# Expert 0's third rows transposed into the bank of the transposed k, and VectorE's lower parts placed ahead of the counts and the list of empty slots

## The chip, the cores and the metric

The kernel runs on one core of a Trainium2 chip. The core has a matrix engine (TensorE, PE in the profile, with its weight loads shown as PEld), a vector engine (VectorE, DVE), a scalar engine (ScalarE, ACT), a general engine (GpSimd, POOL) and an engine that here only issues transfers (SyncE, SP). Each engine works through its own instructions in order, and waits on semaphores for what others have to finish first. The metric is the device time of one execution in microseconds; less is better.

## The reference

Two parts are joined. The first is a retention layer over 8 batches, 8 heads, 576 positions and 64 columns per head: scores q k^T / 8, multiplied by a decay that is zero above the diagonal, times v. The second is a mixture of 8 experts over the 4608 resulting rows of 512 columns; each row goes to the one expert with the largest gating logit.

```python
scores = scale * np.matmul(q, k.transpose(0, 1, 3, 2))
ret = scores * Dmat[None, :, :, :]
attn_out = np.matmul(ret, v)
...
logits = x @ w_gate
e_idx = np.argmax(logits, axis=1)
gate_w = probs[np.arange(N), e_idx]
eom = 1.0 / (1.0 + np.exp(-(x @ w_output_gate)))
for e in range(E):
    mask = e_idx == e
    h = np.maximum(x[mask] @ w1[e], 0.0)
    ye = h @ w2[e]
    out[mask] = gate_w[mask, None] * eom[mask, e, None] * ye
```

## The kernel before

The rows are cut into 36 tiles of 128 (`NTILE`), in groups of four (`GT`), nine groups in all. **Stage one** is the loop over `g` from 0 to 35 (lines 580 to 640). In one turn TensorE forms the scores of tile g+1 into the PSUM tile `sc` (two banks, line 303), the part of tile g that comes from the running state and then the part from its own scores, both into `o_ps` (`by_state`, `outT`), the new state (`update`, not for the last tile of a batch), the transposed k of the next tile into the bank `k_ps` (`k_rows`, not for every tile), and the natural rows and gating logits of tile g-1 into the banks `xa` and `xb` (`xnat`). VectorE masks the scores out of `sc`, scales `o_ps` into `xT`, and adds up the logits. ScalarE empties `xa` and `xb` into `xgrp`.

After every fourth tile a group's gating runs: `gate1a` and `gate1b` find the expert of each row, `gate2` counts ranks on TensorE into the `k_ps` bank, `gate3a` forms the slot of each row, `gate3b` finishes the row's weight and adds the group's counts to `cum`. From the slots GpSimd scatters the group's rows into the DRAM array `xs`, which is sorted by expert (`scatter_x`, line 194, through the list `todo`). Groups 5 and 7 also set `gt["fill"]`, and `gate4` then lists expert 0's empty slots (`fill`, lines 207 to 218), into which GpSimd scatters the zero rows `zx`. The group that this text speaks of is group 7, whose slots are formed in turn 34.

**Stage two** is the experts: the rows come back from `xs`, transposed to columns, and each value is split into a higher part (`xh`, written by ScalarE, line 241) and the remaining lower part (`xl`, written by VectorE, line 245), so that three products replace one. `transp_hi` transposes and writes the higher part, `transp_lo` the lower. `mm1` (line 262) is the first matrix product of an expert, `mm2` (line 283) the second. Expert 0 starts early: the first `TA` = 3 row tiles of its slots (128, 128 and 104 rows) are loaded in turn 31, and transposed in turns 33, 34 and at the start of turn 35. TensorE's transposes go into a PSUM bank that `pools["x_ps"]` names: the `k_ps` bank in turn 33, `sc[:, 1]` in turn 34, `sc[:, 0]` in turn 35.

The order on every engine in the loop is that of the program text (`manual_schedule`). From turn 34 on the order before the change is:

- TensorE: `outT(34)`, `update(34)`, `gate2` of group 7, `xnat(33)`, transposes of rows 1, transposes of rows 2, `by_state(35)`, `outT(35)`, `xnat(34)`, then `mm1(0,0,0)`, `mm1(0,0,1)`, `xnat(35)` and more products.
- VectorE: `xT(34)` (line 422), `gate3a` (lines 478 to 485), logits of tile 33 (540, 541), `gate3b` (495 to 507), `gate4` (515, 207 to 218), `xl` of rows 1, `xl` of rows 2, `xT(35)`, logits of tile 34, then the hidden layer's lower parts (line 270).
- GpSimd: at the end of turn 35 it issues all of `todo` (line 636): four scatters of group 7's rows and three of zero rows, with a memset of a work tile ahead of each.

After the loop `gate3a` and `gate3b` run again for group 8 (lines 709, 710). Line 487 makes its slots (line 485) wait for every scatter issued so far, and the count on TensorE at line 717 needs its `cum` (line 507). The four PSUM buffers `h_ps` of `mm1` lie where the tiles of stage one lay.

Of the kernel before, what the change touches and what calls it, by code (L numbers as in the profile page):

```python
# [10 lines left out]
F32 = mybir.dt.float32  # L11
# [15 lines left out]
P = 128  # L27
NP = H // 2
NTILE = NT // P
# [11 lines left out]
GT = 4  # L41
# [7 lines left out]
def tile_retention_moe(  # L49
# [49 lines left out]
    cum = const.tile([P, E], BF16, name="cum")  # L99
# [5 lines left out]
    def load_rest(step):  # L105
        if step < 3:
            n = slice(P * (step + 2), P * (step + 3))
            SP.dma_start(out=gq_sb[:, :, n], in_=gq[:, :, n])
        if step == 0:
            for p in range(NP):  # L110
                o = 0 if p % 2 == 0 else 16
                A.copy(out=iw[:, p, o:o + P], in_=ident)
        elif step == 1:
            SP.dma_start(out=con_sb[:, CPB * H + 3 * P:], in_=cmat[:, CPB * H + 3 * P:])
        elif step == 2:
            SP.dma_start(out=cbf_sb, in_=cbf)
            SP.dma_start(out=csm_sb, in_=csm)
            SP.dma_start(out=tok_sb, in_=tokid)
            for x in xgrp:
                G.memset(x[:, :, DM:XW], 0.0)  # L120
            G.memset(zx.bitcast(I32)[:, DM:DM + 1], NT)
# [37 lines left out]
    pools = {"xt0": xta, "ht0": hpa}  # L159
# [61 lines left out]
    def transp(e, t):  # L221
        transp_lo(*transp_hi(e, t))

    def transp_hi(e, t):
        part, n = (0, TA * P) if t < TA else (1, CAP - CA)
        t0 = t if part == 0 else t - TA
        if (e, part) not in XT:
            pl = pools[f"xt{part}"]
            XT[e, part] = (pl.tile([P, KB, n], F32R, name=f"xh{part}"), pl.tile([P, KB, n], F32R, name=f"xl{part}"))
        m = ROWS[t] if e == 0 else P  # L230
        hi, lo = (a[:, :, P * t0:P * t0 + m] for a in XT[e, part])
        if e == 0:
            src = pools["x_ps"]()[:, :, :, 0:m]
            for k in range(KB):
                T.transpose(src[:, k // 2, k % 2, :], XG[e, t][0:m, k:DM:KB], ident[0:m, 0:m])
            hi, lo = (a.rearrange("p (b k) i -> p b k i", b=2) for a in (hi, lo))
        else:
            src = pools["xq"].tile([P, KB, P], F32, name="x_t", bufs=2)
            V.transpose(out=src.rearrange("p k (u j) -> p u k j", u=4),
                        in_=XG[e, t].rearrange("p u (i k) -> p u k i", k=KB))  # L240
        A.copy(out=hi, in_=src)
        return src, hi, lo

    def transp_lo(src, hi, lo):
        V.tensor_tensor(out=lo, in0=src, in1=hi.bitcast(F32), op=ALU.subtract)
# [52 lines left out]
    ps_s = psctx.enter_context(tc.tile_pool(name="ps_s", bufs=1, space=PSUM, side="right"))  # L298

    pk, kn, vs, xT, gt = {}, {}, {}, {}, {}  # L300
    st_ps, stcur = [None], [None]

    sc = ps_s.tile([P, 2, 512], F32, name="sc")
# [32 lines left out]
    def load_k(g):  # L336

        if g < NTILE and g % CPB != 8 and by_rows(g):
            kn[g] = wk.tile([P, DM], F32, name="kn")
            SP.dma_start(out=kn[g], in_=krow[g])  # L340

    def k_rows(g):

        if g % CPB == 8 or by_rows(g):
            return
        ps = ps_s.tile([P, NP, P], F32, name="k_ps")
        for p in range(NP):
            T.transpose(ps[:, p, :], pk[g][:, 1, P * p:P * p + P], ident)
        kn[g] = wk.tile([P, DM], F32, name="kn")
        A.copy(out=kn[g], in_=ps.rearrange("p a i -> p (a i)"))  # L350
# [139 lines left out]
    def gate3b():  # L490
        n, oh, ex, zs = gt.pop("pend")
        sli = gt.pop("sl")
        x = xgrp[n % 2]
        es = sm.tile([P, GT, 1], F32, name="es")
        V.tensor_reduce(out=es, in_=ex, op=ALU.add, axis=AX.X)
        V.tensor_scalar(out=es, in0=es, scalar1=1e-9, scalar2=None, op0=ALU.add)
        V.scalar_tensor_tensor(out=zs, in0=zs, scalar=1.0, in1=es, op0=ALU.add, op1=ALU.mult)
        V.tensor_copy(x.bitcast(I32)[:, :, DM:DM + 1],
                      tok_sb[:, n * GT:(n + 1) * GT].rearrange("p (t a) -> p t a", a=1))
        V.reciprocal(out=x[:, :, DM + 1:DM + 2], in_=zs)  # L500

        todo.extend(partial(scatter_x, x[:, t, :], sli[:, t, :]) for t in range(GT))
        if n == 0:
            V.memset(cum, 0.0)
        ohs = sm.tile([P, E], F32, name="ohs")
        V.tensor_reduce(out=ohs, in_=oh.rearrange("p t e -> p e t"), op=ALU.add, axis=AX.X)
        V.tensor_tensor(out=cum, in0=cum, in1=ohs, op=ALU.add)
        if n in (SNAP, NTILE // GT - 2):
            gt["fill"] = n

    def gate4():
        n = gt.pop("fill")
        if n == NTILE // GT - 2:

            V.tensor_tensor(out=cnt[:, 0], in0=cnt[:, 0], in1=bump, op=ALU.add)
            todo.extend(fill(0, 1, cnt[:, 0:1], lim, CT - TA + 1)[0])
        if n == SNAP:

            todo.extend(fill(0, 1, cnt[:, 0:1], float(CA), TA)[0])
            V.tensor_scalar(out=bump, in0=cnt[:, 0], scalar1=-1.0, scalar2=float(CA), op0=ALU.mult, op1=ALU.add)  # L520
            V.tensor_scalar(out=bump, in0=bump, scalar1=0.0, scalar2=None, op0=ALU.max)
            V.tensor_copy(base2, base)
            V.tensor_tensor(out=base2[:, 0, 0:1], in0=base2[:, 0, 0:1], in1=bump, op=ALU.add)
# [42 lines left out]
    gap = const.tile([1, 1], F32, name="gap")  # L566
    every = {mybir.EngineType.PE, mybir.EngineType.Activation, mybir.EngineType.DVE, mybir.EngineType.SP}

    pools["x_ps"] = lambda: ps_s.tile([P, NP, P], F32, name="k_ps").rearrange("p (b k) i -> p b k i", b=2)
    def scatters(n, pause):  # L570
        for f in todo[0:n]:

            G.memset(pause, 0.0)
            f()
        del todo[0:n]

    with tc.manual_schedule():
        S_next = scores(0)
        k_rows(0)
        for g in range(NTILE):  # L580
            S_sb = S_next
            prev = stcur[0] if g % CPB != 0 else None
            if g < 4:
                load_rest(g)
            load_k(g + 1)
            if g < NTILE - 4:
                load(g + 4)
            if g == GT * SNAP + 11:
                first = list(scat)
            if g == GT * SNAP + 11:  # L590
                for t in range(TA):
                    load_rows(0, t, first)
                load_idx(0, 0, first)
            if g == 0:
                outT(g, S_sb, prev)
            if g + 1 < NTILE:
                prep(g + 1)
                S_next = scores(g + 1)
            else:
                pools["x_ps"] = lambda: sc[:, 0].rearrange("p (b k i) -> p b k i", b=2, k=2)  # L600
                transp(0, 2)
            if g < NTILE - 1:

                scatters(2 if GT * SNAP + 6 < g < GT * SNAP + 11 else 1, gap)
            if prev is not None:
                by_state(g, prev)
            weights(g)
            if g > 0:
                outT(g, S_sb, prev)
            update(g)  # L610
            if "pend" in gt and g % GT == 2:

                gate2(ps_s.tile([P, NP, P], F32, name="k_ps").rearrange("p a i -> p (a i)"))
            if g + 1 < NTILE:
                k_rows(g + 1)

            if "half" in gt:
                gate1b()
            if "fill" in gt:
                gate4()  # L620
            if "ps" in gt:
                gate3a()
            weights_lo(g, (0,))
            weights_lo(g - 1, (1,))
            if g > 0:
                xnat(g - 1)
            if "sl" in gt:
                gate3b()
            if "fill" in gt and g == NTILE - 2:
                gate4()  # L630
            if g % GT == 0 and g > 0:
                gate1a(g // GT - 1)
            if g == NTILE - 1:
                wide = wk.tile([P, H, D], F32, name="vp")
            if g == NTILE - 1:
                scatters(len(todo), wide)
            if g in (NTILE - 3, NTILE - 2):
                if g == NTILE - 2:
                    pools["x_ps"] = lambda: sc[:, 1].rearrange("p (b k i) -> p b k i", b=2, k=2)
                transp(0, g - NTILE + 3)  # L640
    gt["after"] = list(scat)
    psctx.close()
    ps_h = mctx.enter_context(tc.tile_pool(name="ps_h", bufs=4, space=PSUM, side="right", reuse_waits="tile"))
# [148 lines left out]
    with ExitStack() as octx:  # L792
        ov = octx.enter_context(tc.tile_pool(name="ov", bufs=1))
        ps_v = octx.enter_context(tc.tile_pool(name="ps_v", bufs=2, space=PSUM))
        n = nc.values_load(ovn[0:1, 0:1], min_val=0, max_val=NOV)  # L795
        with tc.For_i(0, n, 1) as i:
# [3 lines left out]
            x = ov.tile([P, XW], F32, name="ox")  # L800
# [14 lines left out]
            oh = ov.tile([P, FB, P], F32, name="ohT")  # L815
# [83 lines left out]
```

## Time and profile before

| | us |
|---|---|
| median of 3 runs | 612.72 |
| lowest and highest of them | 611.83, 613.25 |
| the profiled execution | 608.3 |
| its span, first to last instruction | 606.5 |
| PE busy in the span | 591.2 |
| DVE busy | 332.0 |
| ACT busy | 221.3 |
| POOL busy | 188.0 |

The span is what the trace covers; the profiled execution took 1.8 us more than that. A row of the timeline gives the start in microseconds from the start of the span, the time taken, the engine, the line, the operation, the tile written and the tiles read, the shape, and in brackets how long the engine had been idle before it and whose work ended that idle time. The view of windows gives the busy time of each engine in a stretch, and the granted clock of TensorE (PEclk), where 1.00 is full speed.

### The profile page before, as it was taken

How to read it: one execution, taken by the hardware profiler on the slowest of the kernel's cores; microseconds unless marked ns; L12 is line 12 of the kernel's file. 1: busy time of each engine (PE TensorE's matmuls, PEld its weight loads, DVE VectorE, ACT ScalarE, POOL GpSimd, SP SyncE). 2: the span in 40 equal slices, each digit the busy share in tenths (PEclk: the TensorE clock that was granted, in tenths of full speed). 3: DMA queues.
4: the chain of work that ended last, by engine and by line, in shares of the span. 5: the costliest groups of instructions: out<-in, count | busy, mean ns of one | idle time of the engine just before them, and what ended most of it. 6: DMA issues, size and time to landing. Idle time of an engine off the chain costs nothing. (4 is left out here: it accounts for less than half of the span.)

```text
span 606.5 us, 13987 instructions
## 1 busy us (share of the span) xinstructions
PE 591.2 (97%) x5688; PEld 529.4 (87%) x5688; DVE 332.0 (55%) x731; ACT 221.3 (36%) x481; POOL 188.0 (31%) x235
## 2 busy tenths in 40 slices
PE   8899999999899999999999999999999999999995
PEld 6789889889798999879978987997899799889974
DVE  3498989898460666625543554445265435625410
ACT  3233444333231544325333443443354344325110
POOL 2245555575636524016013301601250110110011
PEclk9999999999799999999999999999999999999998
DMA  9988999995215676434343634444262335321011
GB/s 312 356 306 329 322 308 328 346 308 165 90 57 192 177 198 194 140 118 135 110 138 116 175 104 136 116 139 139 96 189 91 121 102 146 100 83 52 1 38 42
DMA packets 56925, 100.28 MB, mean 165 GB/s; under 512 B 14839, under 2 KB 35832, under 8 KB 56860
## 3 DMA queue, kind: packets, MB, share of 16 engines
q1 hardware_dynamic: 46988, 76.72, 39.9%
q0 software_dynamic: 9440, 21.60, 9.8%
q8 instruction: 45, 0.74, 0.5%
q10 hardware_dynamic: 432, 1.05, 0.5%
q14 instruction: 20, 0.16, 0.1%
HBM read 77.75 MB, written 31.18 MB: 180 GB/s over the span
## 5 line engine op out<-in xcount | busy, mean ns | idle before, releaser
L262 PE MATMUL h_ps<-xh,w1h 128*128 128x360 f32 (+1 forms) x512 | 155.4, 303 | 0.0
L262 PE MATMUL h_ps<-xh,w1l 128*128 128x360 f32 (+1 forms) x512 | 155.0, 303 | 0.0
L262 PE MATMUL h_ps<-xl,w1h 128*128 128x360 f32 (+1 forms) x512 | 154.9, 303 | 0.0
L289 POOL DMA_INDIRECT out_dram<-y,idx x40 | 39.7, 993 | 314.5 <-ACT y L288 269.5
L270 DVE SCALAR_TENSOR_TENSOR hl<-h_ps,hh 128x360 fp32r<-128x360 f32 (+1 forms) x128 | 61.3, 479 | 129.0 <-ACT hh L269 123.2
L283 PE MATMUL y_ps<-w2h,hh 128*128 128x512 f32 (+1 forms) x320 | 125.1, 391 | 0.0
L283 PE MATMUL y_ps<-w2l,hh 128*128 128x512 f32 (+1 forms) x320 | 125.0, 391 | 0.0
L283 PE MATMUL y_ps<-w2h,hl 128*128 128x512 f32 (+1 forms) x320 | 124.7, 390 | 0.0
L269 ACT ACTIVATE hh<-h_ps 128x360 fp32r<-128x360 f32 (+1 forms) x128 | 54.7, 427 | 118.0 <-PE h_ps L262 117.1
L262 PEld LDWEIGHTS h_ps<-xl,w1h 128*128 128x128 f32 x512 | 96.3, 188 | 0.3
L262 PEld LDWEIGHTS h_ps<-xh,w1h 128*128 128x128 f32 x512 | 96.3, 188 | 0.3
L262 PEld LDWEIGHTS h_ps<-xh,w1l 128*128 128x128 f32 x512 | 96.2, 188 | 0.0
L288 ACT ACTIVATE y<-y_ps,idx 128x512 f32<-128x512 f32 (+1 forms) x40 | 27.5, 688 | 138.8 <-issue 90.1
L147 DVE TENSOR_TENSOR w1l<-st,w1h 128x512 fp32r<-128x512 f32 x64 | 47.3, 776 | 48.2 <-ACT w1h L142 46.8
L283 PEld LDWEIGHTS y_ps<-w2h,hl 128*128 128x128 f32 (+1 forms) x320 | 58.8, 184 | 14.1
L283 PEld LDWEIGHTS y_ps<-w2h,hh 128*128 128x128 f32 (+1 forms) x320 | 58.9, 184 | 13.8
L283 PEld LDWEIGHTS y_ps<-w2l,hh 128*128 128x128 f32 (+1 forms) x320 | 58.8, 184 | 13.6
L354 POOL TENSOR_TENSOR vp<-pk,con_sb 128x512 f32<-128x512 f32 x36 | 37.4, 1040 | 54.5 <-PE st_ps L394 34.9
L194 POOL DMA_INDIRECT xs<-xgrp,sli x36 | 39.0, 1082 | 33.0 <-issue 17.1
L194 POOL DMA_INDIRECT xs<-zx,fill x42 | 45.2, 1077 | 7.1 <-issue 6.6
L147 DVE TENSOR_TENSOR w2l<-st,w2h 128x512 fp32r<-128x512 f32 x64 | 44.7, 736 | 2.3
L378 DVE TENSOR_TENSOR S_sb<-sc,con_sb 128x512 f32<-128x512 f32 x64 | 41.1, 683 | 7.1 <-PE sc L367 6.6
(128 smaller groups left out, 672.4 us busy)
## 6 DMA issues: line engine op xcount, KB each, us to landing
st<-in_w_dram SPq DMA_DIRECT2D x64, 512.0 KB
pk<-in_pack_dram SPq DMA_DIRECT2D x32, 768.0 KB
x_q<-xs SPq DMA_DIRECT2D x140, 64.0 KB
kn<-in_krow_dram SPq DMA_DIRECT2D x14, 256.0 KB
gq_sb<-in_gq_dram SPq DMA_DIRECT2D x5, 256.0 KB
pk<-in_pack_dram SPq DMA_DIRECT2D x4, 256.0 KB
pk<-in_pack_dram SPq DMA_DIRECT2D x2, 512.0 KB
x_g<-xs SPq DMA_DIRECT2D x4, 256.0 KB
```

What stands on the lines that cost most here:

```text
L147: V.tensor_tensor(out=lo[:, k], in0=st[:, k], in1=hi[:, k].bitcast(F32), op=ALU.subtract)
L194: i = G.indirect_dma_start(out=xs, out_offset=bass.IndirectOffsetOnAxis(ap=at, axis=0), in_=x, in_offset=None, **({} if bound is None else ...
L262: i = T.matmul(ps, lhsT=a[:, k, :], rhs=b[:, k, 0:n], start=(j == 0), stop=(j == 3 * KB - 1))
L269: A.activation(out=hh, in_=ps, func=AF.Relu)
L270: V.scalar_tensor_tensor(out=hl, in0=ps, scalar=0.0, in1=hh.bitcast(F32), op0=ALU.max, op1=ALU.subtract)
L283: i = T.matmul(ps, lhsT=a[:, n], rhs=b, start=(j == 0), stop=(j == 3 * FB - 1))
L288: A.activation(out=y, in_=ps, func=AF.Copy, scale=idx.bitcast(F32)[0:m, e, t, 1:2])
L289: G.indirect_dma_start(out=out, out_offset=bass.IndirectOffsetOnAxis(ap=idx[0:m, e, t, 0:1], axis=0), in_=y, in_offset=None, bounds_check= ...
L354: G.tensor_tensor(out=vs[g], in0=pk[g][:, 2].rearrange("p (h d) -> p h d", h=H), in1=gk_sb[:, g % CPB].broadcast_to([P, H, D]), op=ALU.mult)
L378: V.tensor_tensor(out=v(S_sb[:, r].rearrange("p a i -> p (a i)")), in0=v(sc[:, r]), in1=cmat_sb[:, 0:2].rearrange("p c a i -> p a (c i)"). ...
```

## The change

`gate3b` is cut in two. Its end, which adds the group's expert counts to `cum` and sets the mark for the list of empty slots, becomes `gate3c`, called at once except for group 7. For group 7 `gate3b` moves to turn 34's transposes, between `transp_hi` and `transp_lo` of rows 1; `gate3c` and `gate4` move to the end of turn 35, behind `xnat(34)` and just ahead of the scatters. And the transposes of rows 2 at the start of turn 35 go into the `k_ps` bank and no longer into `sc[:, 0]`.

```diff
+        gt["cum"] = (n, oh)
+        if n != NTILE // GT - 2:
+            gate3c()
+
+    def gate3c():
+        n, oh = gt.pop("cum")
         if n == 0:
             V.memset(cum, 0.0)
         ohs = sm.tile([P, E], F32, name="ohs")
...
-    pools["x_ps"] = lambda: ps_s.tile([P, NP, P], F32, name="k_ps").rearrange("p (b k) i -> p b k i", b=2)
+    def k_bank():
+        return ps_s.tile([P, NP, P], F32, name="k_ps").rearrange("p (b k) i -> p b k i", b=2)
+
+    pools["x_ps"] = k_bank
+
...
             else:
-                pools["x_ps"] = lambda: sc[:, 0].rearrange("p (b k i) -> p b k i", b=2, k=2)
+                pools["x_ps"] = k_bank
                 transp(0, 2)
...
-            if "sl" in gt:
+            if "sl" in gt and g != NTILE - 2:
                 gate3b()
-            if "fill" in gt and g == NTILE - 2:
-                gate4()
             if g % GT == 0 and g > 0:
                 gate1a(g // GT - 1)
             if g == NTILE - 1:
                 wide = wk.tile([P, H, D], F32, name="vp")
-            if g == NTILE - 1:
+                gate3c()
+                gate4()
                 scatters(len(todo), wide)
             if g in (NTILE - 3, NTILE - 2):
                 if g == NTILE - 2:
                     pools["x_ps"] = lambda: sc[:, 1].rearrange("p (b k i) -> p b k i", b=2, k=2)
-                transp(0, g - NTILE + 3)
+                x = transp_hi(0, g - NTILE + 3)
+                if "sl" in gt:
+                    gate3b()
+                transp_lo(*x)
```

## The prediction

> **What bounds the kernel now.** I read the page first, then TensorE's waits, then its timeline around the one long wait, then the granted clock there.
>
> ```profile
> span 606.5 us, 13987 instructions
> PE 591.2 (97%) x5688; PEld 529.4 (87%) x5688; DVE 332.0 (55%) x731; ACT 221.3 (36%) x481; POOL 188.0 (31%) x235
> PEclk9999999999799999999999999999999999999998
> ```
>
> TensorE is busy for 97% of the span: what shortens its chain shortens the kernel. Its clock is full in every slice but one in the middle, the eleventh (151.6 to 166.8 us). The waits of TensorE from 138 us to the end, the whole answer:
>
> ```profile
> PE sc L235 <- DVE xl L245: 3.0, 1, 3.0
> PE t_ps L717 <- DVE cum L507: 0.2, 1, 0.2
> ```
>
> One wait of 3.0 us: transposes (line 235) wait for VectorE's lower parts (line 245). After it TensorE waits 0.2 us in 440. So nothing behind 156 us has slack on TensorE to swallow a gain, and loads and scatters that TensorE's progress releases move with it. The place itself, in TensorE's timeline (first a usual turn, then the wait):
>
> ```profile
> 147.04 0.66 PE L531 MATMUL xa<-iw,xT 128*128 128x144 f32 x4
> 148.02 0.67 PE L235 MATMUL k_ps<-con_sb,x_g 128*128 128x128 f32 x4
> 148.61 0.90 PE L367 MATMUL sc<-pk 64*64 64x128 f32 x32
> 149.33 0.62 PE L409 MATMUL o_ps<-pk,stT 64*64 64x128 f32 x16
> 149.88 1.09 PE L418 MATMUL o_ps<-S_sb,vp 128*64 128x128 f32 x16
> 150.81 0.64 PE L394 MATMUL st_ps<-vp,kn 128*64 128x64 f32 x16
> ...
> 151.64 0.74 PE L531 MATMUL xa<-iw,xT 128*128 128x144 f32 x4
> 152.70 0.64 PE L235 MATMUL sc<-con_sb,x_g 128*128 128x128 f32 x4
> 156.30 0.97 PE L235 MATMUL sc<-con_sb,x_g 104*128 104x104 f32 x4 [2.96 <-DVE xl L245]
> ...
> 162.08 0.60 PE L262 MATMUL h_ps<-xh,w1h 128*128 128x360 f32 x1
> 162.51 0.33 PE L262 MATMUL h_ps<-xl,w1h 128*128 128x360 f32 x1
> 162.68 0.33 PE L262 MATMUL h_ps<-xh,w1l 128*128 128x360 f32 x1
> ```
>
> Rows 1 are transposed at 152.70, rows 2 only at 156.30, after 2.96 us idle. And what follows the wait is slow: four transposes take 0.97 us, in the usual turn 0.67. The view of windows says why:
>
> ```profile
> 19.07:22.48 3.41, 2.08 (x60) 1.43 (x52) 1.78 (x4) 0.18 (x1) 0.35 (x1) 1.00 1.09 317
> ...
> 152.20:155.61 3.41, 1.14 (x10) 0.94 (x8) 2.96 (x22) 1.33 (x3) 0.56 (x1) 1.00 0.02 5
> 155.61:159.02 3.41, 2.72 (x28) 2.14 (x30) 1.23 (x3) 0.51 (x1) 3.08 (x5) 0.50 0.42 159
> 159.02:162.44 3.42, 3.42 (x21) 3.09 (x18) 0.87 (x2) 0.37 (x1) 3.09 (x5) 0.50 0.40 158
> 162.44:165.85 3.41, 3.41 (x23) 3.41 (x22) 0.71 (x2) 0.84 (x2) 3.08 (x5) 1.00 0.21 79
> ```
>
> The columns are PE, PEld, DVE, ACT and POOL busy, then the clock. It is half, 0.50, for 6.83 us from 155.61, that is from 2.3 us into the wait, and full again at 162.44. So the wait is paid twice.
>
> Why so long? VectorE at that time:
>
> ```profile
> 152.48 0.15 DVE L480 COPY cnt<-k_ps 128x1 f32<-128x1 f32 x1
> 153.40 0.17 DVE L541 TENSOR_TENSOR lg<-xb,lg 128x16 f32<-128x16 f32 x1
> 154.19 0.18 DVE L506 TENSOR_REDUCE ohs<-oh 128x8 f32<-128x32 bf16 x1
> 155.48 0.16 DVE L218 TENSOR_TENSOR fill<-fl,csm_sb 128x3 int32<-128x3 f32 x1
> 155.56 0.68 DVE L245 TENSOR_TENSOR xl<-sc,xh 128x512 fp32r<-128x512 f32 x1
> 157.84 0.59 DVE L245 TENSOR_TENSOR xl<-sc,xh 128x416 fp32r<-128x416 f32 x1 [1.60 <-ACT xh L241]
> ```
>
> The lower parts of rows 1 run from 155.56 to 156.24, and TensorE starts 0.06 us later. Though rows 2 go into the other half of `sc`, the transposes wait for the last reader of that tile. Ahead of it VectorE has eight small instructions, from line 506 at 154.19 to line 218.
>
> **The change, part by part.**
>
> *The bank.* Rows 2 now go into `k_ps`. Its last readers are `gate3a`'s, line 480 the last, done at 152.48 + 0.15 = 152.63. A usual set of four transposes takes 148.61 - 148.02 = 0.59, so TensorE is through rows 1 at 152.70 + 0.59 = 153.29, after the bank is free: no wait. From there to the first product the trace of usual turns gives each step by the distance of starts: transposes 0.59, `by_state` 149.88 - 149.33 = 0.55, `outT` 150.81 - 149.88 = 0.93, `xnat` 148.02 - 147.04 = 0.98; sum 3.05. The first product starts at 153.29 + 3.05 = 156.34 and the second 0.17 later (162.68 - 162.51), at 156.51 against 162.51. That is **6.00 us** less in this execution: 2.96 of wait, the other 3.04 of half clock.
>
> *The order on VectorE.* For the first product all lower parts must be there. The five instructions of `gate3b` stay behind line 541 and end where line 506 began, at 154.19. Then come `xl` of rows 1 and 2; ScalarE's higher part of rows 1 was ready in time:
>
> ```profile
> 153.37 0.58 ACT L241 CAST xh<-sc 128x512 fp32r<-128x512 f32 x1
> ```
>
> Rows 1's `xl` ends at 154.87. Rows 2 are transposed by 153.9, their higher part follows on ScalarE until about 154.5, so their `xl` ends at 154.87 + 0.59 = 155.46, 0.9 us before TensorE wants it. Were the eight instructions left in place, it would end at 156.24 + 0.59 = 156.83 and hold TensorE for 0.5 us; that is the worth of the move by itself. The `xT(35)` of VectorE follows `outT(35)` (155.4) and ends by about 156.2, before any product could want that bank.
>
> *What is put late.* The eight instructions, 155.56 - 154.19 = 1.37 us, come behind the logits of tile 34. Those of tile 33 came (line 541 at 153.40) 1.76 us after their `xnat` started at 151.64. `xnat(34)` would start at 155.36, so line 541 ends by 157.3 and the list of empty slots is there by 158.7. Who wants it is GpSimd, which issues group 7's rows first and one work-tile memset ahead of each:
>
> ```profile
> 155.05 0.96 POOL L194 DMA_INDIRECT xs<-xgrp,sli  x1 [3.01 <-issue]
> ...
> 161.73 1.00 POOL L194 DMA_INDIRECT xs<-zx,fill  x1 [0.16 <-issue]
> ...
> 165.14 0.98 POOL L194 DMA_INDIRECT xs<-zx,fill  x1 [0.16 <-issue]
> DMA to landing us min/median/max: 2.7/2.8/2.9
> 174.50 0.17 DVE L485 CAST sli<-slf 128x4 int32<-128x4 f32 x1 [0.21 <-DVE slf L483]
> ```
>
> The first zero rows go out at 161.73, 3.0 us after the list: free by that cover. `gate3b` ends when it did, so the first scatter keeps its 155.05, and GpSimd, at its own pace, ends this run of seven scatters where it does today. That is the one thing which does **not** move 6 us forward. The last is issued at 165.14 and lands 2.8 us on, at 167.9. Group 8's slots (line 485, now 174.50) wait for that landing and would come at 168.5: 0.6 us to spare. If that cover is gone, `cum`, then line 717 on TensorE, wait one for one. No queue of SP is passed.
>
> **From this execution to the median.** The span would be 606.5 - 6.0 = 600.5. The median of the runs shown, 612.72, is 4.4 above the 608.3 of the profiled one; nothing in the views says where that lies. The 2.96 of wait comes from instructions on two engines and should be the same in every run. The clock's part need not: half clock for one stretch of 3.41 us in place of two would cost 1.7 and not 3.04, and the three runs lie 1.42 apart. For the median I take the middle of these ends, 2.4. An end of zero stays too: at 19.07 to 22.48 TensorE was idle for 1.33 of 3.41 us (39%) and kept 1.00, at 152.20 to 155.61 for 2.27 (67%) and lost it. So a wait of 2.96 that fell evenly on two such stretches might cost no clock. Forecast: 612.72 - 2.96 - 2.4 = **607.3**; its own range is 606.2 to 608.4.
>
> The Trainium skill, "TensorE: Matmul & The Clock Gate", Part 1: The HAM clock gate, says that the clock falls to half after at least one idle window of about 3.4 us, and that the windows run freely, not from the kernel's start. The first speaks against half of this gain: 2.96 us is shorter, and by it only the wait would go, 609.8. This trace disagrees, it shows 0.50 behind 2.96 us; that the windows lie elsewhere in other executions no run here shows.
>
> **Rivals.**
>
> 1. *Only the wait counts.* In the timed runs the clock seldom drops, or drops for less: the gain is the 2.96, 609.8. For it: the 39% row above. Against: the profiled execution, the fastest time shown, had the full drop. Chance 0.13.
> 2. *A shorter wait takes its place*, behind `outT` or the first product (the lower parts of rows 2, `xT(35)` in a bank of `h_ps`). By my sum they are 0.9 and 0.1 us early; late by 1 to 1.5 they would leave a gain of 4 to 5 with the clock kept, about 3 if it drops for one stretch. Chance 0.05, time 609.
> 3. *It doesn't do what it says*: the transposes of rows 2 still wait for the lower parts of rows 1, through something other than `sc`. These end at 154.87 now, so the wait is 1.6 us and the half clock may stay: gain 1.3, 611.4. That TensorE took `k_ps` at 148.02 and for `gate2` without any wait speaks against. Chance 0.06.
> 4. *Slower*: the list comes late, so the zero rows do, and line 485 holds VectorE and line 717 TensorE. The price is one for one beyond the 0.6 us to spare, and about 1.7 to 3 more once a new gap costs the clock. It breaks even where the last landing is some 3.6 us later (3 of wait and 3 of clock against 6), that is at 171.5, the list at 158.7 + 3.0 + 3.6 = 165.3. At a list 2 us later still it costs 2 us: 614.7. Only `xnat(34)` 6 us late would do that. Chance 0.03.
>
> **The numbers.** Forecast 0.73, and the rivals 0.13, 0.05, 0.06 and 0.03. A measurement of this kernel tells about 0.2%, 1.2 us, from no change. Faster by more: 0.73 + 0.13 + 0.05 and half of rival 3 = 0.94, which I lower to 0.92; within: 0.05; slower: 0.03. The range reaches from 605.8 (the 6.0 of this execution and 0.9 of spread below the median) to 610.2 (rival 1 and the lower end of no clock loss, with 0.4 of spread).
>
> **What would show it.** Right: after rows 1 the transposes into `k_ps` start at once, no wait of TensorE over 0.3 us between 150 and 165, clock 1.00 in all windows there, the first product near 156.3, VectorE's line 506 behind line 541 of tile 34, the first zero rows still at 161.7, line 485 near 168.5 with TensorE at line 717 waiting about 0.2. Wrong: an `[... <-DVE ...]` at the transposes or the first product, 0.50 anywhere behind 150, or a wait at line 717 that has grown.

## The result and the profile after

The changed kernel took 607.53 us in the median of 6 runs (607.05 to 609.33), the kernel before 611.85 in 6 runs: ratio 0.9919, 95% interval 0.9897 to 0.9940. That is 4.3 us in the medians, and the forecast was 607.3. Two more weighings of the same pair, on chips A and C below (the record names no chip for the first), gave 606.59 against 611.21 (0.9926, 0.9913 to 0.9940) and 607.55 against 612.16 (0.9931, 0.9910 to 0.9952): 4.6 us both times.

The whole answer of TensorE's waits from 140 us to the end, for the changed kernel:

```profile
PE t_ps L729 <- DVE cum L513: 0.2, 1, 0.2
```

The 3.0 us at the transposes are gone, and no other wait has come. The 0.2 is the old one at the count of group 8 (line 717 before, 729 now). TensorE's timeline at the same place (start, us, engine, line, operation, out<-in):

```profile
157.31 0.63 PE L235 MATMUL sc<-con_sb,x_g 128*128 128x128 f32 x4
157.78 0.63 PE L235 MATMUL k_ps<-con_sb,x_g 104*128 104x104 f32 x4
158.34 0.67 PE L409 MATMUL o_ps<-pk,stT 64*64 64x128 f32 x16
158.94 1.09 PE L418 MATMUL o_ps<-S_sb,vp 128*64 128x128 f32 x16
159.96 0.76 PE L537 MATMUL xa<-iw,xT 128*128 128x144 f32 x4
160.56 0.65 PE L537 MATMUL xb<-iw,xT 128*128 128x144 f32 x4
160.95 0.42 PE L262 MATMUL h_ps<-xh,w1h 128*128 128x360 f32 x1
161.21 0.33 PE L262 MATMUL h_ps<-xl,w1h 128*128 128x360 f32 x1
```

Rows 2 follow rows 1 without a gap, into `k_ps`, and every step runs at its usual speed. From the start of the transposes of rows 1 to the second product it is now 161.21 - 157.31 = **3.90 us**, where the first trace had 162.51 - 152.70 = 9.81. The clock in the view of windows (PE, PEld, DVE, ACT, POOL busy, then the granted clock):

```profile
157.30:161.20 3.90, 3.90 (x51) 3.46 (x50) 3.17 (x14) 1.83 (x5) 1.51 (x2) 1.00 0.02 4
161.20:168.00 6.80, 6.80 (x45) 6.80 (x44) 3.93 (x20) 2.29 (x6) 6.07 (x8) 1.00 0.43 165
```

By these two traces alone the place gives 5.9 us. Yet the spans differ by 1.0 only, 605.5 against 606.5. Most of the rest is there before the place: rows 1 were transposed at 152.70 in the first trace and at 157.31 in this one, 4.6 us later, though the two programs give TensorE the same instructions up to there. Which of the two is usual had to be seen from further traces of both kernels.

### The profile page after: what moved, and what is told of

Same layout as the page of the kernel before. It is cut to its first block, busy times and chain, and to the rows that moved or that the text cites. A ratio compares the mean times of both kernels' runs of the same rounds, so it can differ in the third digit from the quotient of the medians.

```text
span 605.5 us, 13987 instructions
## 1 busy us (share of the span) xinstructions
PE 593.1 (98%) x5688; PEld 529.9 (88%) x5688; DVE 330.0 (54%) x731; ACT 220.4 (36%) x481; POOL 188.8 (31%) x235
## 5 line engine op out<-in xcount | busy, mean ns | idle before, releaser
L147 DVE TENSOR_TENSOR w1l<-st,w1h 128x512 fp32r<-128x512 f32 x64 | 44.0, 725 | 48.1 <-ACT w1h L142 46.8
L354 POOL TENSOR_TENSOR vp<-pk,con_sb 128x512 f32<-128x512 f32 x36 | 38.9, 1082 | 58.2 <-PE st_ps L394 36.2
```

The lines of the kernel that those rows point to most:

```text
L147: V.tensor_tensor(out=lo[:, k], in0=st[:, k], in1=hi[:, k].bitcast(F32), op=ALU.subtract)
L354: G.tensor_tensor(out=vs[g], in0=pk[g][:, 2].rearrange("p (h d) -> p h d", h=H), in1=gk_sb[:, g % CPB].broadcast_to([P, H, D]), op=ALU.mult)
```

## The experiments

Below, "the place" is the time from the start of the transposes of rows 1 to the start of the second product, read from the timeline as above. The runs were made in three sets, each on a chip of its own.

| kernel | chip | median, us | before, same chip | ratio, 95% interval | the place, us |
|---|---|---|---|---|---|
| before, again | A | 610.87 | 611.21 | 0.9995 (0.9974 to 1.0017) | 8.76 |
| bank only | A | 606.94 | 611.21 | 0.9928 (0.9914 to 0.9941) | 4.11 |
| order only | A | 609.44 | 611.21 | 0.9971 (0.9959 to 0.9984) | 5.74 |
| changed, again | A | 606.59 | 611.21 | 0.9926 (0.9913 to 0.9940) | 3.90 |
| filled wait | B | 606.45 | 607.07 | 0.9980 (0.9960 to 0.9999) | 7.14 |
| zero rows 2.3 late | B | 604.70 | 607.07 | 0.9968 (0.9946 to 0.9989) | 3.90 |
| zero rows 4.2 late | B | 607.37 | 607.07 | 1.0002 (0.9984 to 1.0019) | 3.90 |
| changed, third | C | 607.55 | 612.16 | 0.9931 (0.9910 to 0.9952) | 3.90 |
| filled wait, again | C | 610.30 | 612.16 | 0.9972 (0.9957 to 0.9987) | 7.14 |
| zero rows 2.3 late, again | C | 609.32 | 612.16 | 0.9960 (0.9940 to 0.9979) | 3.90 |

**The kernel before, again** (no edit).

> The kernel before, unchanged, for a second trace and its clock in the timed runs. Theory (a wait of 3.0 us that costs the clock as well): the wait at the transposes of rows 2 is 2.9 to 3.0 us again, since it comes from two engines' own instructions; the half clock behind it lasts one or two stretches of 3.4 us, by where they lie (1.7 to 3.1 us lost), so the mean granted clock differs between runs; stage one (start of the turn-34 transposes, 152.7 us in the first trace) moves by several us from execution to execution, which would explain why the changed kernel's trace, 4.6 us later at that place with the same instructions, ends only 1.0 us earlier. Rival (the change itself slows stage one by 4.6 us): this trace has rows 1 transposed at 152.7 us again, within 0.5. Ratio 1.000.

TensorE's timeline, and the windows behind the wait:

```profile
156.70 0.64 PE L235 MATMUL sc<-con_sb,x_g 128*128 128x128 f32 x4
160.30 0.73 PE L235 MATMUL sc<-con_sb,x_g 104*128 104x104 f32 x4 [2.97 <-DVE xl L245]
160.96 0.67 PE L409 MATMUL o_ps<-pk,stT 64*64 64x128 f32 x16
161.56 1.88 PE L418 MATMUL o_ps<-S_sb,vp 128*64 128x128 f32 x16
...
165.46 0.33 PE L262 MATMUL h_ps<-xl,w1h 128*128 128x360 f32 x1
```

```profile
160.30:162.00 1.70, 1.70 (x26) 1.43 (x28) 0.39 (x1) 0.51 (x1) 1.53 (x3) 0.91 0.41 159
162.00:163.70 1.70, 1.70 (x15) 1.37 (x12) 0.41 (x2) 0.00 (x0) 1.53 (x3) 0.50 0.44 159
163.70:165.40 1.70, 1.70 (x9) 1.70 (x9) 0.66 (x2) 0.37 (x1) 1.53 (x3) 0.58 0.40 159
```

The wait is the same to a hundredth, 2.97. The clock is not: it is still full when TensorE resumes (line 409 takes its usual 0.67), falls about 1.4 us later (0.91 over 1.7 us is 0.31 us at half, so from 161.7), and is back near 165.1. That is one stretch of 3.4 us where the first trace had 6.83. The place takes 8.76 for 9.81. And rows 1 come at 156.70 with the old kernel too: the rival that the change slows stage one falls. The places of rows 1 go with the chip: 156.3 to 156.9 in four traces on chip A, 151.9 to 152.8 in three on B, 156.8 to 158.4 in three on C, whatever the kernel. The expectation had stage one move by several us from execution to execution; here it moves by 1.6 us at most on one chip, and by more between chips. As each chip had one set of runs, chip and set can't be told apart.

**The bank only.**

```diff
-                pools["x_ps"] = lambda: sc[:, 0].rearrange("p (b k i) -> p b k i", b=2, k=2)
+                pools["x_ps"] = lambda: ps_s.tile([P, NP, P], F32, name="k_ps").rearrange("p (b k) i -> p b k i", b=2)
                 transp(0, 2)
```

> Only the bank: rows 2 are transposed into the bank of k_ps, the eight instructions of the counts and the list stay ahead of the lower parts. Theory: the transposes follow at once; the lower parts of rows 2 come at about the time of the old order, and the first product waits some 0.5 us for them; the clock stays at 1.00. So nearly the whole gain: 4.0 to 5.0 us faster than before, at most 0.6 us behind the whole change. Rival (the order on VectorE is what counts): the wait only moves to the first product, 2 us or more, and at most half the gain is kept.

TensorE, then VectorE:

```profile
156.88 0.64 PE L235 MATMUL sc<-con_sb,x_g 128*128 128x128 f32 x4
157.36 0.63 PE L235 MATMUL k_ps<-con_sb,x_g 104*128 104x104 f32 x4
...
160.59 0.40 PE L262 MATMUL h_ps<-xh,w1h 128*128 128x360 f32 x1
160.99 0.44 PE L262 MATMUL h_ps<-xl,w1h 128*128 128x360 f32 x1
```

```profile
159.76 0.68 DVE L245 TENSOR_TENSOR xl<-sc,xh 128x512 fp32r<-128x512 f32 x1
160.36 0.58 DVE L245 TENSOR_TENSOR xl<-k_ps,xh 128x416 fp32r<-128x416 f32 x1
```

With the small instructions still in front, the last lower part ends at 160.94, and the second product, the first to read a lower part, starts at 160.99. The first product reads the higher parts alone and does not wait. So the old order costs 4.11 - 3.90 = 0.21 us and not 0.5: the second product starts 0.40 after the first and not 0.26, which is 0.14 of it; the other 0.07 lies ahead of the first product, without a wait in the trace. In the medians it is 0.35, within their spread. The bank does nearly all of it.

**The order only**: the changed kernel, with rows 2 in `sc` again.

```diff
             else:
-                pools["x_ps"] = k_bank
+                pools["x_ps"] = lambda: sc[:, 0].rearrange("p (b k i) -> p b k i", b=2, k=2)
                 transp(0, 2)
```

> Only the order: the lower parts ahead of the counts and the list, but rows 2 still in sc[:, 0]. Theory: the transposes of rows 2 still wait for the lower parts of rows 1, now 1.6 us (1.4 to 1.8) in place of 2.96. If the clock holds at 1.00 behind 1.6 us of idle time, it is 3 to 4 us faster than before; if it falls as behind 2.96, about 1.4 us faster. Rival (rows 2 wait for something other than sc's last reader): the wait is gone, or still 3 us.

```profile
156.58 0.63 PE L235 MATMUL sc<-con_sb,x_g 128*128 128x128 f32 x4
158.79 0.73 PE L235 MATMUL sc<-con_sb,x_g 104*128 104x104 f32 x4 [1.58 <-DVE xl L245]
...
162.32 0.33 PE L262 MATMUL h_ps<-xl,w1h 128*128 128x360 f32 x1
158.80:162.30 3.50, 3.50 (x45) 3.06 (x46) 1.31 (x3) 0.88 (x2) 3.03 (x5) 1.00 0.25 97
```

The wait is 1.58, to where the lower parts of rows 1 now end: it is the last reader of the other half of `sc` that rows 2 wait for. In this trace the clock stayed at 1.00. In the six runs it seems to have done so only at times: their mean clocks are 0.994 three times and 0.996 to 0.997 three times. (The trace without a drop at the place has 0.997: the clock falls to half at TensorE's idle end of the span, some 3 us there.) So the kernel stood between the two answers expected: 1.8 us faster than before, and 2.85 slower than the changed kernel, of which 5.74 - 3.90 = 1.84 is the place. That the other 1.0 is the clock's part is not shown: the three runs at 0.994 took 609.19 to 609.54 us, the three above it 608.38, 609.77 and 609.87, so the runs with the lower clock were not the slower ones.

**The changed kernel again.**

> The changed kernel again, beside the two halves on the same chip. Theory: no wait of TensorE over 0.3 us between the transposes and the first product, clock 1.00 there, 4.3 to 5.2 us faster than before in the median, ratio 0.9915 to 0.993; from the start of the transposes of rows 1 to the first product 3.7 us in every trace. Rival (the gain is luck of stage one): under 3 us.

3.90 us at the place, clock full there, 4.62 us faster than before, as expected.

**The wait filled with work**: the kernel before, with three products into the free bank. Their result is read by nobody, and nothing else is changed.

```diff
+                busy = ps_s.tile([P, NP, P], F32, name="k_ps").rearrange("p a i -> p (a i)")
+                for _ in range(3):
+                    T.matmul(busy, lhsT=ident, rhs=gq_sb[:, 0, 0:512], start=True, stop=True)
                 pools["x_ps"] = lambda: sc[:, 0].rearrange("p (b k i) -> p b k i", b=2, k=2)
                 transp(0, 2)
```

> The kernel before, with three matrix products whose result nobody reads set into the wait of 3.0 us (128x512, float32, into the free bank of k_ps, some 2.6 us by the distance of xnat's products); all else as before, the wait's end included. Theory (half of the cost is the clock, not the wait): rows 2 are transposed as late as before, but the clock stays at 1.00, so the kernel is 1.7 to 2.1 us faster than before though it does more; from the transposes of rows 1 to the second product 6.8 to 7.0 us, where the kernel before had 9.81 in one trace and 8.76 in another. Rival (the clock falls for another reason, or costs nothing in the median): same as before, or slower by what the products add.

```profile
152.80 0.64 PE L235 MATMUL sc<-con_sb,x_g 128*128 128x128 f32 x4
153.27 2.74 PE L602 MATMUL k_ps<-gq_sb,con_sb 128*128 128x512 f32 x6
156.40 0.73 PE L235 MATMUL sc<-con_sb,x_g 104*128 104x104 f32 x4 [0.39 <-DVE xl L245]
...
159.94 0.33 PE L262 MATMUL h_ps<-xl,w1h 128*128 128x360 f32 x1
152.80:156.40 3.60, 3.21 (x12) 1.43 (x10) 3.10 (x19) 1.04 (x3) 1.25 (x2) 1.00 0.02 5
156.40:160.00 3.60, 3.60 (x46) 3.15 (x47) 1.40 (x3) 0.91 (x3) 3.27 (x5) 1.00 0.40 150
```

Rows 2 are transposed 3.60 us after rows 1, as before. But what follows runs at full speed, and the place takes 7.14 against 8.76 and 9.81. A kernel that does more work was faster: by 0.62 us in the medians on chip B, not the 1.7 to 2.1 expected, and its interval (0.06 to 2.4 us) hardly fixed the size. So it ran again beside the changed kernel on chip C:

> The changed kernel on the same chip as the next two, to weigh them against it. Theory: 4.3 to 5 us faster than the kernel before (2.96 of wait and 1.4 to 2 of clock). Rival (the gain belongs to one chip): under 3.5 us or over 6.

> The kernel before with its wait filled by three products, again: its first interval, 0.06 to 2.4 us faster than before, was too wide to size the clock. Theory: 1.2 to 2 us faster than before, and 2.9 to 3.2 slower than the changed kernel (the wait itself, which it keeps). Rival (the clock costs little in the median): under 0.8 faster, and 3.6 or more slower than the changed kernel.

There the kernel with the filled wait is 1.86 us faster than before, and the changed kernel a further 2.75. That parts the gain of 4.61: **1.86 for the clock, 2.75 for the wait** (2.97 in the traces). The interval of the first is 0.8 to 2.6 us, so the clock's part is clear of zero on both chips but not fixed to better than about 1 us. Why the median of chip B gave less stays open; the two intervals overlap, and one of its twelve runs has a mean clock of 0.994 though the wait was filled.

**The list of empty slots late.** One more memset of the work tile ahead of each zero-row scatter, or of all seven scatters, of group 7; the computation is as in the changed kernel.

```diff
-        for f in todo[0:n]:
+        for j, f in enumerate(todo[0:n]):
 
-            G.memset(pause, 0.0)
+            for _ in range(2 if n > 4 and j >= 4 else 1):
+                G.memset(pause, 0.0)
             f()
```

The second leaves out `and j >= 4`.

> The changed kernel with one more memset of the work tile ahead of each of the three zero-row scatters of group 7, 0.7 us each, so that the last lands 2.1 us later. Theory (0.6 us to spare): group 8's slots (line 485) wait for the landing, 1.5 us (1.2 to 1.8), TensorE waits as long at line 729 on top of its 0.2, and the kernel is 1.4 to 2 us slower than the changed one, up to 1.7 more in runs in which the clock falls. Rival (the landing is far from binding): no change, line 729 waits 0.2.

> The same with one more memset ahead of each of all seven scatters: the last lands 4.9 us later. Theory: line 485 and with it line 729 wait 4.3 us (4.0 to 4.6), the clock falls in every run since the wait is longer than a stretch of 3.41 us, and costs 1.7 to 3 more: 6 to 7 us slower than the changed kernel, 1 to 3 slower than before. Rival: no change, or one for one without the clock (4.3).

TensorE's wait and VectorE's at group 8's slots, first with the three, then with the seven:

```profile
PE t_ps L730 <- DVE cum L513: 2.2, 1, 2.2
DVE sli L485 <- DMA xs<-zx,fill: 2.2, 1, 2.2
```

```profile
PE t_ps L730 <- DVE cum L513: 3.4, 1, 3.4
DVE sli L485 <- DMA xs<-zx,fill: 3.4, 1, 3.4
172.16 0.19 PE L730 MATMUL t_ps<-cum,cbf_sb 128*128 128x8 bf16 x1 [3.40 <-DVE cum L513]
168.00:171.50 3.50, 0.76 (x5) 0.46 (x3) 0.49 (x4) 0.24 (x1) 1.30 (x2) 0.88 0.01 0
171.50:174.50 3.00, 2.34 (x9) 2.34 (x10) 2.93 (x12) 0.47 (x1) 1.61 (x2) 0.50 0.00 0
174.50:178.00 3.50, 3.50 (x15) 3.50 (x14) 1.24 (x5) 0.47 (x1) 2.68 (x3) 0.57 0.60 232
```

Now the landing of the zero rows binds, and TensorE stands as long as VectorE. From the first scatter to the last it was 169.78 - 159.68 = 10.10 us in the changed kernel, 167.02 - 154.58 = 12.44 with three memsets more: 2.34 later, 2.0 of them waited for. So 0.3 us were to spare. With seven it is 4.23 later (168.54 - 154.21 = 14.33) and 3.2 waited for, 1.0 to spare; line 485 came 2.4 us after the last issue there and 3.1 with three, so the spare time moves with the landing. Both waits came out otherwise than expected, 2.0 for 1.5 and 3.2 for 4.3. The three memsets ran beside the changed kernel on chip C:

> The changed kernel with its zero rows 2.3 us later, again beside the changed kernel: the trace had line 730 wait 2.2 us in place of 0.2. Theory: 2.0 to 2.6 us slower than the changed kernel, 2 of wait and the clock in the few runs in which it falls. Rival (a wait there is taken back later): within 0.8.

It cost 1.77 us, under the 2.0 to 2.6 expected, with a wait of 1.8 in its trace, 1.6 more than the changed kernel has. So the wait there is paid in full, as far as twelve runs from 608.15 to 612.97 can say. With seven memsets the kernel is where the kernel before was, 607.37 for 607.07, and not 1 to 3 us slower as expected; the changed kernel itself did not run on chip B. That the clock would fall in every run was wrong by the mean clocks: at a wait of 3.4 us it shows 0.50 in the trace, for 6.8 us, but two of ten runs have a mean clock of 0.998.

## Why the prediction was right, and where its size was off

*Where the time was.* Right: TensorE bounds the kernel, the one long wait was its whole loss behind stage one, and nothing later swallowed the gain.

*The bank.* Right. The transposes follow at once; line 480, the last reader of `k_ps`, was done at 157.26, ahead of the transposes of rows 1 at 157.31. The chain was worked out as 156.51 - 152.70 = 3.81 and measured 3.90.

*The order on VectorE.* The times were right and one reading was not. The lower parts were to end 2.76 us after rows 1 started and ended at 2.66. But the 0.5 us that the old order would have cost was put on the first product; the second is the first to read a lower part, and 0.21 was measured.

*What was put late.* Right. VectorE and GpSimd in the changed kernel:

```profile
157.11 0.15 DVE L480 COPY cnt<-k_ps 128x1 f32<-128x1 f32 x1
158.82 0.66 DVE L245 TENSOR_TENSOR xl<-sc,xh 128x512 fp32r<-128x512 f32 x1
159.39 0.58 DVE L245 TENSOR_TENSOR xl<-k_ps,xh 128x416 fp32r<-128x416 f32 x1
163.12 0.17 DVE L218 TENSOR_TENSOR fill<-fl,csm_sb 128x3 int32<-128x3 f32 x1
159.68 0.97 POOL L194 DMA_INDIRECT xs<-xgrp,sli  x1 [3.02 <-ACT xh L241]
166.37 1.00 POOL L194 DMA_INDIRECT xs<-zx,fill  x1 [0.17 <-DVE lg L546]
169.78 0.99 POOL L194 DMA_INDIRECT xs<-zx,fill  x1 [0.16 <-issue]
173.17 0.17 DVE L485 CAST sli<-slf 128x4 int32<-128x4 f32 x1 [0.21 <-DVE slf L483]
```

Counted from rows 1, the list was to be there at 6.0 us and was at 5.98 (163.29); the first zero rows go out at 9.06, forecast 9.03; line 485 comes at 15.86, forecast 15.8, and is not held up. The cover was real but thin: 0.6 us by the median landing, 0.3 to 1.0 by the experiments. What the fourth rival would have needed is seen in the kernel with seven memsets, which has lost the whole gain.

*The size.* That 607.53 lies so near the forecast of 607.3 is in part luck. The forecast took 5.4 us off 612.72, the median of three runs; the median of six is 611.85, 0.9 lower, and the gain from there is 4.3. The two errors nearly cancel. The term of the sum that was too big is the one for the clock. The traces have the two ends that it named, 9.81 at the place for two stretches of half clock and 8.76 for one. For the median I took their middle, 2.4. The experiment that removes only the clock's part gives 1.86 on one chip and 0.62 on another, and the gain in medians is 4.3 to 4.6, not 5.4. The mean clocks of 78 runs of the kernel before show how its runs divide:

| mean clock | 0.989 to 0.992 | 0.993 to 0.995 | 0.996 to 0.999 |
|---|---|---|---|
| runs | 20 | 44 | 14 |

One stretch of 3.41 us at half takes 3.41 x 0.5 / 606 = 0.003 off the mean, and the traces without a drop lie at 0.996 to 0.998. So by this estimate about a quarter of the runs had two stretches, over half had one, and a fifth none: with 2.7, 1.6 and 0 us (9.81, 8.76 and nothing against 7.14) that is some 1.6 on average. The borders of the classes are rough, since the idle end of the span takes some 0.002 to 0.004 off as well. But the times agree in direction, each class 1.1 to 2.7 us faster than the one to its left: among the runs of the kernel before that ran beside the experiments, the medians of the three classes are 613.05, 611.00 and 609.40 us (the last a single run) on chip A, 609.83, 607.11 and 605.72 on B, 613.15, 611.87 and 610.72 on C. Of 17 runs of the changed kernel none is below 0.995. The first rival, that only the wait counts, holds for that fifth.

When it is one stretch and when two, three traces suggest and do not prove. Where the clock fell inside the wait, with some idle time still to come, it stayed at half for 6.8 us: in the first trace (fall at 155.61, end of the wait at 156.30) and with seven memsets (170.66 and 172.16). Where it fell after the wait, in the second trace of the kernel before, it was back after 3.4.

The first trace, at 608.3 for 612.72 in the median, was a fast one in stage one, like those of chip B. Its span was the wrong thing to compare; the place was the right one.

By the idle window of the Trainium skill's page, "TensorE: Matmul & The Clock Gate", Part 1: The HAM clock gate, the clock's part of this gain should not have been there. The traces disagree: the clock fell 2.3 us into the wait of the first trace and 1.9 us into that of the kernel with seven memsets (170.66 - 168.76), before any 3.4 us of idle time had passed. By the mean clocks it fell in most runs of the kernel before, with its 2.97 us. That its windows run freely agrees with them: the same wait was followed by a fall at 2.3 us into it in one trace, and 1.4 us after its end in another.

## What to carry to other kernels

A wait of the bounding engine is to be priced twice: by its length, and by what the clock does behind it, which here varied between runs of one program; a trace shows one case of it, and the mean clocks of the timed runs tell how common it is. Before a bank is shared, look at which reader a writer really waits for: here the other half of a tile was enough to hold TensorE for 3 us, while another bank was free: that one line was worth 4.3 of the 4.6 us. And when work is moved later, follow it to whoever waits for its landing: here 0.3 to 1.0 us were left of a cover that would have cost the whole gain had the landing come some 4 us later.

## What was not expected of the hardware

By the mean clocks alone, the clock fell in half of six runs behind an idle time of only 1.58 us (0.994, where the trace without a drop has 0.997), and stayed full in two of ten runs (0.998) of a kernel whose trace had 3.4 us of it. Products whose result nobody reads, set into a wait, made the kernel 1.86 us faster (ratio 0.9972, 0.9957 to 0.9987), by keeping the clock alone: 1.00 in both of its traces, and rows 2 transposed as late as before. And the length of stage one went with the chip, or with the set of runs on it, by 3.5 to 6.5 us at the same instructions (rows 1 at 151.9 to 152.8 on one, 156.3 to 158.4 on the others).
